# Attention's state as one plane of 64x64 tiles, the gates' chain split between VectorE and GpSimd, and another fixed order

## The chip, the cores and the metric

The kernel runs on one core of a Trainium2 chip. The metric is device time in microseconds (us) of one launch, as the median of several runs. A core has TensorE (PE; PEld is its weight load), VectorE (DVE), ScalarE (ACT), GpSimd (POOL) and SyncE (SP), which only issues DMA transfers here.

## The reference, cut to what matters

Three layers follow one another: a gated linear attention (mLSTM) over 2 batches of 8 heads with 768 steps and head size 40, then two feed-forward layers over all 1536 tokens (320 wide, 2048 and 1536 hidden).

```python
for t in range(S):                       # attention, per batch and head
    m_new = np.maximum(f_gate[:, :, t] + m, i_gate[:, :, t])
    f_stab = np.exp(f_gate[:, :, t] + m - m_new)
    i_stab = np.exp(i_gate[:, :, t] - m_new)
    m = m_new
    C = f_stab * C + i_stab * outer(vt, kt)      # state, 40 x 40
    n = f_stab * n + i_stab * kt                 # its 41st column
    h_tilde = C @ qt;  nq = n . qt
    y[t] = sigmoid(o_gate[t]) * h_tilde / max(|nq|, 1)
...
h = x @ w_in                             # layer 1
g = (a0 + a1 h + a2 h^2 + a3 h^3) / (1 + |b0| |h| + |b1| h^2 + 1e-6)
x = g @ w_out
...
xn = x / rms(x) * rms_g                  # layer 2
out = (silu(xn @ w_gate) * (xn @ w_val)) @ w_out
```

## The kernel before, in words

**Order.** The program first makes a list of small pieces by calls of `task(key, fn, deps, take, give)`; a piece has a key such as `("yi", 3)` and its instructions. Nothing is issued then. `run` (L184) walks through the hand-fixed table `ORDER`, a list of the pieces' numbers, and issues each piece's instructions. Each engine executes its own instructions in that order, so `ORDER` fixes every engine's queue and SP's queue of transfers. A piece may take a buffer from a ring and give it back; the eight PSUM banks are one ring, `"b"`, and a piece gets the bank that was given back longest ago.

**Gates.** Rows 0 to 15 and 32 to 47 of small tiles hold one row for each batch and head. The 768 steps are cut in two parts, a=0 (256 steps) and a=256 (512 steps). `gm` scans m (DVE, L423); `ga` makes two sums for the forget gate (DVE, L430 and L431); `gi` makes one for the input gate (POOL, L434); `gb` takes exponentials (ACT, L437, L438); `gc` splits the forget factor in two f16 words (DVE, L441); `gd` runs one cumulative product for each chunk of 128 steps (DVE, L449, whose second input `zc` is a zero in SBUF); `ge` transposes the result to `idt` (PE, then a copy on DVE).

**Attention** goes in 12 chunks j of 128 steps (6 for each batch). In a chunk: `s` products of k and q (PE, L504), `f` spreads the gates (PE, L484), `scan` makes the decay matrix (DVE, L487), `a` weighs the products by it (DVE, L509), `vp` and `v2` weigh v (POOL, L494, L515), `y` is the part inside the chunk (PE, L537), `yi` the part of the earlier state (PE, L527), `ys` scales that (DVE, L531), `yd` adds the two (DVE, L541), `u` is the state's growth (PE, L549), `cd` decays the state (POOL, L555), `ca` adds (DVE, L563, L565). `den0`, `den1`, `den` (ACT, POOL, DVE) make the denominators from the 41st column, `rs` and `xm` multiply (POOL), `xt`, `xh`, `xl` transpose into `xall` for layer 1. In the first chunk of a batch there is no `yi`, `ys` or `cd`, in the last one no `u`, `cd` or `ca`.

The state `cst` is a tile of 128 partitions x 4 pairs of heads x 2 planes x 41. A pair's first head has partitions 0 to 39 of plane 0, its second one partitions 64 to 103 of plane 1; all else is zero. `yi` contracts all 128 partitions, 8 products in all, with 64 columns of q as weights and both planes (82 columns) as the moving side:

```python
PE.matmul(out=t[c, 2 * p:2 * p + 2], lhsT=T("lqk", j)[:, 0, p, c], rhs=cst[:, p])
```

So the rows of the q tile between the heads have to be zero, for which `setup` clears them on POOL (L409), and the state too (L410).

**Layer 1** has 48 pairs i of (256 tokens, 256 hidden columns): `in0`, `in1` (PE, L676), a chain of elementwise pieces on ACT, DVE and POOL (`hu`, `z`, `p1`, `h2`, `zu`, `p2`, `p3`, `ars`, `sq`, `w`, `y2`, `g`, and for pairs from 16 on `gh`, `gl`), and `out0`, `out1` (PE, L681, L695, L697). Weights arrive as 64-bit words and are taken apart by `c0`, `c1`, `c2` (DVE, L331, L337, L343; `cr` on ACT and an addition on POOL for some), `hi` (ACT) and a subtraction on POOL. **Layer 2** runs in blocks of 512 or 256 tokens: `g0`, `g1` (PE, L865), `silu`, `mul`, `sh`, `sl`, and `out2` (PE, L873 to L875), then the rows go out.

## Time and profile before

| what | value |
|---|---|
| time, median of 3 runs | 481.06 us (480.97 to 481.06) |
| the profiled execution: its time, its span | 481.12 us, 479.3 us |
| PE busy | 456.4 us, 95% of the span |
| DVE, ACT, POOL busy | 331.1, 304.8, 317.5 us |
| chain of waits that ended last | PE 65%, ACT 14%, POOL 9%, DVE 8% |

The span is the time from the first to the last instruction of the program that the profile shows; the execution's own time holds 1.8 us more. Busy PE is not PE at its peak, as the ends of matmuls are modelled. An fp32 product leaves two MATMUL records, an fp32r or f16 one leaves one.

### The profile page before, as it was taken

Reading aid. Unit: us, or ns where it says so; the run is one execution under the profiler, and the core shown is the slowest. Engines: PE = TensorE matmul, PEld = TensorE weight load, DVE = VectorE, ACT = ScalarE, POOL = GpSimd, SP = SyncE. Lnnn points to the kernel's source line nnn. Section 1 sums busy time; section 2 is a strip of 40 time slices with the busy share of each in tenths; the row PEclk is TensorE's granted clock in tenths of the full one; section 3 lists DMA queues with packets and bytes.
Section 4 is the critical chain, followed back from the end, with each engine's and each line's share of the span. In section 5 each row is a group of like instructions: output and inputs, shape, how many; then the busy total and the mean of one; then the engine's idle time right before and its main releaser. Section 6 shows DMA issues by size and latency. Waiting matters only on the chain.

```text
span 479.3 us, 9356 instructions
## 1 busy us (share of the span) xinstructions
PE 456.4 (95%) x3552; PEld 414.5 (86%) x3552; DVE 331.1 (69%) x609; ACT 304.8 (64%) x576; POOL 317.5 (66%) x337
## 2 busy tenths in 40 slices
PE   3699899989999999999999999999999999999996
PEld 2588778778789999999999988888898889999996
DVE  7999999999999989899999999875210210201211
ACT  3245999999998899799999988552422212212311
POOL 5689999999998898886977778990831303213320
PEclk9998999999999999999999999999999999999999
DMA  8869371325032060010322144571100000000001
GB/s 239 273 204 255 101 196 31 114 61 143 1 102 63 1 203 3 1 42 2 115 90 83 38 160 166 180 233 59 34 15 27 1 0 2 1 27 29 1 14 57
DMA packets 18366, 40.41 MB, mean 84 GB/s; under 512 B 3952, under 2 KB 11904, under 8 KB 18320
## 3 DMA queue, kind: packets, MB, share of 16 engines
q1 hardware_dynamic: 18320, 39.80, 27.4%
q8 instruction: 28, 0.46, 0.4%
q14 instruction: 18, 0.15, 0.1%
HBM read 35.86 MB, written 3.93 MB: 83 GB/s over the span
## 4 chain that ended last, share of the span: by engine, by line
PE 65%; ACT 14%; POOL 9%; DVE 8%; issue 3%; DMA 1%; POOLq 0%; DVEq 0%; ACTq 0%
PE bank L865 26%; PE bank L676 10%; PE bank L695 5%; PE bank L875 4%; PE bank L873 4%; PE bank L874 4%; PE bank L681 4%; POOL z L720 2%; PE bank L697 2%; ACT z L710 2%; ACT u L709 2%; ACT bank L732 2%; ACT vv L718 1%; DVE w_buf L487 1%; POOL cv L356 1%
## 5 line engine op out<-in xcount | busy, mean ns | idle before, releaser
L676 PE MATMUL bank<-xall,win 128*128 128x256 f32 x768 | 104.0, 289 | 3.5 <-ACT yb L543 1.6
L676 PEld LDWEIGHTS bank<-xall,win 128*128 128x128 f32 x768 | 96.5, 193 | 7.1 <-ACT yb L543 1.8
L941 DVE TENSOR_TENSOR vv<-bank,vv 128x512 f32<-128x512 f32 x35 | 23.6, 688 | 98.0 <-PE bank L865 97.8
L720 POOL TENSOR_TENSOR z<-z,u 128x512 f32<-128x512 f32 x48 | 62.0, 1292 | 14.1 <-ACT z L710 13.1
L947 POOL TENSOR_TENSOR wou<-vv,wou 128x512 fp32r<-128x512 f32 x16 | 20.7, 1295 | 53.7 <-ACT wou L944 49.4
L938 ACT ACTIVATE vv<-bank 128x512 f32<-128x512 f32 x35 | 20.7, 595 | 50.6 <-PE bank L865 46.2
L865 PE MATMUL bank<-xall,w2gv 128*128 128x512 f32 (+1 forms) x256 | 46.4, 337 | 0.0
L749 POOL TENSOR_TENSOR gl<-vv,gh 128x512 fp32r<-128x512 f32 x32 | 41.3, 1296 | 5.6 <-ACT gh L748 3.8
L865 PEld LDWEIGHTS bank<-xall,w2gv 128*128 128x128 f32 x256 | 39.2, 190 | 4.7 <-DVE vv L739 0.2
L710 ACT ACTIVATE z<-u,few 128x512 f32<-128x512 f32 x48 | 39.2, 816 | 1.0
L695 PE MATMUL bank<-wou,gh 128*128 128x320 f32 x128 | 38.9, 316 | 0.0
L697 PE MATMUL bank<-wou,gh 128*128 128x320 f32 x128 | 38.0, 309 | 0.0
L681 PE MATMUL bank<-scr,vv 128*128 128x320 f32 x128 | 37.1, 435 | 0.0
L737 DVE SCALAR_TENSOR_TENSOR bank<-vv,few,bank 128x512 f32<-128x512 f32 x48 | 35.8, 749 | 0.0
L735 DVE SCALAR_TENSOR_TENSOR z<-z,bank 128x512 f32<-128x512 f32 x48 | 32.6, 682 | 4.4 <-ACT bank L734 3.6
L732 ACT ACTIVATE bank<-z,few 128x512 f32<-128x512 f32 x48 | 32.9, 686 | 2.5 <-DVE vv L729 2.5
L739 DVE SCALAR_TENSOR_TENSOR vv<-z,bank 128x512 f32<-128x512 f32 x48 | 32.6, 683 | 0.6
L331 DVE TENSOR_SCALAR bank<-raw 128x320 int32<-128x320 int32 x68 | 32.6, 486 | 0.3
L709 ACT ACTIVATE u<-bank 128x512 f32<-128x512 f32 x48 | 28.7, 598 | 4.0 <-POOL z L720 1.8
L865 PE MATMUL bank<-win,w2gv 128*128 128x512 f32 x128 | 31.1, 391 | 0.0
L681 PEld LDWEIGHTS bank<-scr,vv 128*128 128x128 f32 x128 | 23.2, 190 | 8.2 <-DVE vv L739 0.2
L364 POOL TENSOR_TENSOR win<-cv,win 64x128 fp32r<-64x128 f32 (+2 forms) x37 | 28.0, 757 | 2.4 <-ACT win L360 0.5
(169 smaller groups left out, 1180.3 us busy)
## 6 DMA issues: line engine op xcount, KB each, us to landing
raw<-in_w_out_dram SPq DMA_DIRECT2D x14, 640.0 KB, 4.1
raw<-in_w_gv_dram SPq DMA_DIRECT2D x12, 640.0 KB, 4.3
raw<-in_w_in_dram SPq DMA_DIRECT2D x8, 640.0 KB, 5.8
lqk<-in_qk_tr_dram SPq DMA_DIRECT2D x24, 192.0 KB, 4.7
los<-in_o_gate_dram SPq DMA_DIRECT2D x12, 160.0 KB, 3.6
lv<-in_v_dram SPq DMA_DIRECT2D x12, 160.0 KB, 4.3
lk<-in_k_dram SPq DMA_DIRECT2D x12, 160.0 KB, 3.8
z_dram<-rnd SPq DMA_DIRECT2D x6, 320.0 KB, 4.8
```

Source lines behind the costliest of these rows:

```text
L331: DVE.tensor_scalar(out=mid(x), in0=word(x, 1), scalar1=3, scalar2=0x3FFFFFFF, op0=ALU.logical_shift_left, op1=ALU.bitwise_and,)
L676: PE.matmul(out=hb()[:, e], lhsT=l, rhs=r, start=(x == 0), stop=(x == len(mm) - 1))
L681: PE.matmul(out=T("acc", n, t)[:, 0:DM], lhsT=T("vv", i)[:, e, t * 128:(t + 1) * 128], rhs=w[:, e], start=p + e == 0, stop=p == NPAIR - 1 ...
L695: PE.matmul(out=o, lhsT=l, rhs=woh[:, e], start=first, stop=last)
L697: PE.matmul(out=o, lhsT=l, rhs=wol[:, e], start=False, stop=False)
L709: go("hu", lambda: ACT.activation(out=u(), in_=hb(), func=ACTF.Abs), [("in1", i)], ["u"])
L710: go("z", lambda: ACT.activation(out=z(), in_=u(), func=ACTF.Identity, scale=babs[:, 1:2], bias=babs[:, 0:1]), [("hu", i)], ["z"])
L720: go("zu", lambda: POOL.tensor_tensor(out=z(), in0=z(), in1=u(), op=ALU.mult), [("z", i)], [], ["u"])
L732: go("ars", lambda: ACT.activation(out=hb(), in_=z(), func=ACTF.Abs_reciprocal_sqrt, bias=cq), [("zu", i), ("p3", i)])
L737: go("y2", lambda: DVE.scalar_tensor_tensor(out=hb(), in0=vv(), scalar=nacoef[:, 0:1], in1=hb(), op0=ALU.add, op1=ALU.mult), [("w", i)])
L749: go("gl", lambda: POOL.tensor_tensor(out=gl(), in0=vv(), in1=r32(gh()), op=ALU.subtract), [("gh", i)], ["gl"], ["vv"])
L865: PE.matmul(out=bank(i, e), lhsT=l, rhs=r, start=y == 0, stop=y == len(mm) - 1)
```

## The change

- **State.** `cst` becomes one plane, 128 x 4 x 41: the pair's first head on partitions 0 to 39, its second on 64 to 103. `yi` makes 16 products instead of 8, each contracting 40 partitions for one head with 64 columns of q as weights and 41 moving columns, in the four 64x64 tiles of the array; the two heads of a pair go to two PSUM banks, so `yi` takes two banks instead of one. `ys` reads them with two instructions instead of one. `u` writes 64 rows instead of 40 for each head: its weights are 64 columns of k, of which the last 24 belong to the next head (or, behind the last head, to 24 cleared columns). `cd` and `ca` become one instruction over 128 partitions instead of two over 40.
- **Cleared tiles.** The clearing of q's rows, of `cst` and of `zc` on POOL goes; two 24-column strips behind k are cleared instead.
- **Gates.** `gi` is joined to `ga`. For part a=0 all three sums run on DVE, for a=256 all three on POOL. The zero that `gd` reads moves from SBUF to a word of the PSUM bank into which `ge` of the same part transposes; DVE clears it, and `gd` takes the bank instead of `ge`.
- **Order.** `ORDER` is another list of all 1946 pieces (two `gi` fewer than before). `LAG` is 0, so `PAIRS` is the same list as before.

Read with the pieces' names, the two orders compare so (pieces that issue instructions, counted from the table; the joined `ga` counts once):

| ahead of `in0` of pair | DVE | ACT | POOL | PE | DVE's `c0`, `c1`, `scan`, `yd` |
|---|---|---|---|---|---|
| 0, before | 65 | 26 | 30 | 29 | 13, 12, 9, 2 |
| 0, after | 59 | 23 | 28 | 26 | 11, 9, 8, 3 |
| 8, before | 127 | 81 | 60 | 65 | 21, 21, 12, 4 |
| 8, after | 128 | 76 | 56 | 65 | 22, 22, 12, 4 |
| 24, before | 247 | 196 | 120 | 150 | 32, 32, 19, 7 |
| 24, after | 251 | 200 | 119 | 150 | 32, 32, 19, 7 |

Ahead of pair 8, and ahead of pair 24, PE has the same pieces in both orders, in another sequence. ACT's functions change in the order's sequence so that its table has to change 10 times before and 12 times after. The transfer of q and k for chunk 0 moves from the fourth place of SP's queue to the second, ahead of the first weights.

```diff
--- before.py
+++ after.py
@@ -20,101 +20,102 @@
 OB = [["ob"] * 4, ["raw", "raw", "raw", "ob"], ["ob", "raw"], ["ob", "cv"]]
 F_CV = [1] * 16 + [0] * 18
 NATIVE = [0, 1, 2, 3, 4, 5, 6, 7, 8, 9, 10, 11, 12, 13, 14, 15]
+LAG = 0
 BY_SQUARE = [0, 2, 4, 6, 8, 10, 12, 14, 16, 18, 20, 22, 24, 26, 28]
 ORDER = [
...
 ]
 
 
@@ -162,7 +163,8 @@
 
     BLOCKS = [(0, 2 * BLK), (2 * BLK, 2 * BLK), (4 * BLK, BLK), (5 * BLK, BLK)]
 
-    PAIRS = [(n, p) for p in range(NPAIR) for n in range(2)] + [(n, p) for n in range(2, NB) for p in range(NPAIR)]
+    PAIRS = [(n, x - n * LAG) for x in range(NPAIR + LAG) for n in range(2) if 0 <= x - n * LAG < NPAIR]
+    PAIRS += [(n, p) for n in range(2, NB) for p in range(NPAIR)]
     FINAL = [max(i for i, x in enumerate(PAIRS) if x[0] == n) for n in range(NB)]
 
     PE, ACT, DVE, POOL = nc.tensor, nc.scalar, nc.vector, nc.gpsimd
@@ -265,13 +267,12 @@
     dexp = at.tile([48, NCH, BH // 2], FP32, name="dexp")
     idt = at.tile([128, NCH, 48], FP32, name="idt")
     dl = at.tile([128, NCH, BH // 2], FP32, name="dl")
-    cst = at.tile([128, HP, 2, D1], FP32, name="cst")
-    zc = at.tile([48, 1], FP32, name="zc")
+    cst = at.tile([128, HP, D1], FP32, name="cst")
     den = at.tile([128, H, 1], FP32, name="den")
-    for nm, n in (("k", 2), ("v", 2)):
-        ring("l" + nm, tiles(at, n, [128, H, D], FP32, "l" + nm))
-    qk_bufs = tiles(at, 2, [128, 2, HP, L], FP32, "lqk")
-    ring("lqk", qk_bufs)
+    ring("lv", tiles(at, 2, [128, H, D], FP32, "lv"))
+    lk_bufs = tiles(at, 2, [128, H * D + 64 - D], FP32, "lk")
+    ring("lk", lk_bufs)
+    ring("lqk", tiles(at, 2, [128, 2, HP, L], FP32, "lqk"))
     ring("yb", tiles(at, 2, [128, H, D1], FP32, "yb"))
 
 
@@ -282,7 +283,10 @@
     def load(i, nm):
         if nm != "qk":
             src = {"k": k, "v": v, "o": o_gate}[nm][i * L:(i + 1) * L].rearrange("p (h d) -> p h d", h=H)
-            nc.sync.dma_start(out=lo_of(i) if nm == "o" else T("l" + nm, i), in_=src)
+            dst = lo_of(i) if nm == "o" else T("l" + nm, i)
+            if nm == "k":
+                dst = dst[:, 0:H * D].rearrange("p (h d) -> p h d", h=H)
+            nc.sync.dma_start(out=dst, in_=src)
             return
         for e in range(2):
             nc.sync.dma_start(
@@ -403,11 +407,8 @@
         DVE.memset(g48, 0.0)
         DVE.memset(cq, 1.0 + 1e-6)
         DVE.memset(eps6, 1e-6)
-        POOL.memset(zc, 0.0)
-        for t in qk_bufs:
-            for r0 in (32, 96):
-                POOL.memset(t[r0:r0 + 32, 0], 0.0)
-        POOL.memset(cst, 0.0)
+        for t in lk_bufs:
+            POOL.memset(t[:, H * D:], 0.0)
         for nm, dst, src in (
             ("eye", ident, eye4[:, 0:128]), ("eye4", id4, eye4), ("sel", sel, pick), ("hv", hv[FR], halves),
             ("pb", bcoef, pb[None, :].to_broadcast([128, 2])), ("pa", acoef, pa[None, :].to_broadcast([128, 4])),
@@ -426,12 +427,11 @@
         )
 
     def gate_a(a, b):
-        gf = gate_in[:, 0, a:b]
-        DVE.tensor_tensor(out=gf, in0=gf, in1=m_t[:, a:b], op=ALU.add)
-        DVE.tensor_tensor(out=g48[FR, a:b], in0=gf, in1=m_t[:, a + 1:b + 1], op=ALU.subtract)
-
-    def gate_i(a, b):
-        POOL.tensor_tensor(out=g48[0:BH, a:b], in0=gate_in[:, 1, a:b], in1=m_t[:, a + 1:b + 1], op=ALU.subtract)
+        e = POOL if a else DVE
+        gf, m1 = gate_in[:, 0, a:b], m_t[:, a + 1:b + 1]
+        e.tensor_tensor(out=gf, in0=gf, in1=m_t[:, a:b], op=ALU.add)
+        e.tensor_tensor(out=g48[FR, a:b], in0=gf, in1=m1, op=ALU.subtract)
+        e.tensor_tensor(out=g48[0:BH, a:b], in0=gate_in[:, 1, a:b], in1=m1, op=ALU.subtract)
 
     def gate_b(a, b):
         ACT.activation(out=g48[:, a:b], in_=g48[:, a:b], func=ACTF.Exp)
@@ -444,9 +444,11 @@
         DVE.memset(f16[:, a:b].rearrange("p (c l) -> p c l", l=L)[:, :, 0:1], 0.0)
 
     def gate_d(a, b):
+        zc = T("gt", a)[FR, 511:512]
+        DVE.memset(zc, 0.0)
         for c in range(a // L, b // L):
             sl = g48[FR, c * L:(c + 1) * L]
-            DVE.tensor_tensor_scan(out=sl, data0=sl, data1=zc[FR].to_broadcast([BH, L]), initial=1.0, op0=ALU.mult, op1=ALU.add)
+            DVE.tensor_tensor_scan(out=sl, data0=sl, data1=zc.to_broadcast([BH, L]), initial=1.0, op0=ALU.mult, op1=ALU.add)
 
     def gate_e(a, b):
         c0, c1 = a // L, b // L
@@ -521,14 +523,22 @@
             return T(name, j)[:, 0:H * D1].rearrange("p (h d) -> p h d", h=H)
 
         def yi():
-            t = heads("pi")
             for p in range(HP):
                 for c in (slice(0, 64), slice(64, 128)):
-                    PE.matmul(out=t[c, 2 * p:2 * p + 2], lhsT=T("lqk", j)[:, 0, p, c], rhs=cst[:, p])
+                    for e in range(2):
+                        r = slice(64 * e, 64 * e + D)
+                        PE.matmul(out=odd(e)[c, p], lhsT=T("lqk", j)[r, 0, p, c], rhs=cst[r, p])
+
+        def odd(e):
+            return T("pi", j, e)[:, 0:HP * D1].rearrange("p (a b) -> p a b", a=HP)
 
         def ys():
-            dd = idt[:, ch, 32 + b * H:32 + (b + 1) * H][:, :, None].to_broadcast([128, H, D1])
-            DVE.tensor_tensor(out=T("yb", j), in0=heads("pi"), in1=dd, op=ALU.mult)
+            dd = idt[:, ch, 32 + b * H:32 + (b + 1) * H].rearrange("p (a e) -> p a e", e=2)
+            for e in range(2):
+                DVE.tensor_tensor(
+                    out=T("yb", j).rearrange("p (a e) d -> p a e d", e=2)[:, :, e], in0=odd(e),
+                    in1=dd[:, :, e:e + 1].to_broadcast([128, HP, D1]), op=ALU.mult,
+                )
 
         def y():
             t = heads("py")
@@ -546,23 +556,18 @@
             t = T("pu", j)[:, 0:HP * D1].rearrange("p (a b) -> p a b", a=HP)
             for h in range(H):
                 r0 = 64 * (h % 2)
-                PE.matmul(out=t[r0:r0 + D, h // 2], lhsT=T("lk", j)[:, h], rhs=v2_buf[:, h])
+                PE.matmul(out=t[r0:r0 + 64, h // 2], lhsT=T("lk", j)[:, h * D:h * D + 64], rhs=v2_buf[:, h])
 
         def cd():
-            for e in range(2):
-                r = slice(64 * e, 64 * e + D)
-                dd = dl[r, ch, b * HP:(b + 1) * HP][:, :, None].to_broadcast([D, HP, D1])
-                POOL.tensor_tensor(out=cst[r, :, e, 0:D1], in0=cst[r, :, e, 0:D1], in1=dd, op=ALU.mult)
+            dd = dl[:, ch, b * HP:(b + 1) * HP][:, :, None].to_broadcast([128, HP, D1])
+            POOL.tensor_tensor(out=cst, in0=cst, in1=dd, op=ALU.mult)
 
         def ca():
             t = T("pu", j)[:, 0:HP * D1].rearrange("p (a b) -> p a b", a=HP)
-            for e in range(2):
-                r = slice(64 * e, 64 * e + D)
-                cc = cst[r, :, e, 0:D1]
-                if ch:
-                    DVE.tensor_tensor(out=cc, in0=t[r], in1=cc, op=ALU.add)
-                else:
-                    DVE.tensor_copy(out=cc, in_=t[r])
+            if ch:
+                DVE.tensor_tensor(out=cst, in0=t, in1=cst, op=ALU.add)
+            else:
+                DVE.tensor_copy(out=cst, in_=t)
 
         def den_(x):
             if x == 0:
@@ -612,8 +617,10 @@
             ("v2", j), None if last else v2, [("scan", j, 0), ("scan", j, 1), ("vp", j)] + prev("u")
         )
         if ch:
-            task(("yi", j), yi, [("s", j), ("ca", j - 1)], take=[key_(("pi", j))], give=[("lqk", j)])
-            task(("ys", j), ys, [("yi", j), ("gates", ch)], take=[("yb", ("yb", j))], give=[("pi", j)])
+            task(("yi", j), yi, [("s", j), ("ca", j - 1)], take=[key_(("pi", j, e)) for e in range(2)],
+                 give=[("lqk", j)])
+            task(("ys", j), ys, [("yi", j), ("gates", ch)], take=[("yb", ("yb", j))],
+                 give=[("pi", j, e) for e in range(2)])
         task(("y", j), y, [("a", j, 0), ("a", j, 1), ("vp", j)], take=[key_(("py", j))])
         task(
             ("yd", j), yd, [("y", j)] + ([("ys", j)] if ch else []),
@@ -984,13 +991,11 @@
 
             go("gm", lambda a=a, b=b: gate_m(a, b),
                [("ld", "gates")] + ([("gm", parts[x - 1][0])] if x else []))
-            go("gi", lambda a=a, b=b: gate_i(a, b), [("gm", a)])
             go("ga", lambda a=a, b=b: gate_a(a, b), [("gm", a)])
-            go("gb", lambda a=a, b=b: gate_b(a, b), [("ga", a), ("gi", a)])
+            go("gb", lambda a=a, b=b: gate_b(a, b), [("ga", a)])
             go("gc", lambda a=a, b=b: gate_c(a, b), [("gb", a)])
-            go("gd", lambda a=a, b=b: gate_d(a, b), [("gc", a)])
-            go("ge", lambda a=a, b=b: gate_e(a, b), [("gd", a), ("ld", "eye")], take=[("b", ("gt", a))],
-               give=[("gt", a)])
+            go("gd", lambda a=a, b=b: gate_d(a, b), [("gc", a)], take=[("b", ("gt", a))])
+            go("ge", lambda a=a, b=b: gate_e(a, b), [("gd", a), ("ld", "eye")], give=[("gt", a)])
             for c in range(a // L, b // L):
                 task(("fgates", c), None, [("gc", a), ("ld", "sel"), ("ld", "eye4")])
                 task(("gates", c), None, [("ge", a)])
```

## Rows read from the trace of the kernel before

**Rows 1.** Windows: length, busy us of PE, PEld, DVE, ACT, POOL.
```profile
0.00:15.40 15.40, 4.92 (x29) 3.88 (x29) 12.38 (x25) 5.04 (x9) 7.75 (x14) 1.00 0.89 246
15.40:44.90 29.50, 26.45 (x331) 22.95 (x330) 28.54 (x59) 13.63 (x30) 25.15 (x39) 0.98 0.78 240
44.90:60.00 15.10, 13.65 (x149) 12.49 (x148) 14.25 (x26) 12.65 (x24) 14.04 (x22) 0.93 0.47 133
60.00:120.00 60.00, 56.20 (x432) 46.44 (x429) 57.19 (x101) 57.78 (x102) 58.39 (x58) 1.00 0.37 109
120.00:300.00 180.00, 179.54 (x1519) 165.51 (x1518) 170.27 (x308) 165.93 (x321) 151.29 (x155) 1.00 0.23 71
300.00:475.64 175.64, 175.60 (x1106) 163.19 (x1104) 48.50 (x95) 49.33 (x95) 60.88 (x53) 1.00 0.14 45
```

**Rows 2.** Timeline of PE (start us, us, what): layer 1's first pair.
```profile
44.90 3.16 PE L676 MATMUL bank<-xall,win 128*128 128x256 f32 x16
```

**Rows 3.** Timeline of DVE, 3 to 16.5 us: the gates' chain.
```profile
5.24 0.78 DVE L430 TENSOR_TENSOR scr<-scr 16x256 f32<-16x256 f32 x1
6.05 1.20 DVE L431 TENSOR_TENSOR scr<-scr 16x256 f32<-16x256 f32 x1
7.28 0.68 DVE L430 TENSOR_TENSOR scr<-scr 16x512 f32<-16x512 f32 x1
7.99 0.68 DVE L431 TENSOR_TENSOR scr<-scr 16x512 f32<-16x512 f32 x1
...
10.04 0.41 DVE L441 SCALAR_TENSOR_TENSOR f<-scr,f 16x256 f16<-16x256 f32 x1
...
10.61 0.73 DVE L449 TENSOR_TENSOR_SCAN scr<-scr,zc 16x128 f32<-16x128 f32 x2
...
12.72 2.65 DVE L449 TENSOR_TENSOR_SCAN scr<-scr,zc 16x128 f32<-16x128 f32 x4
```

**Rows 4.** Timeline of POOL, 3 to 20 us: what ran beside rows 3.
```profile
4.25 2.71 POOL L434 TENSOR_TENSOR scr<-scr 16x256 f32<-16x256 f32 x2
12.83 1.63 POOL L356 TENSOR_TENSOR cv<-cv,rnd 128x640 int32<-128x640 int32 x1 [5.86 <-DVE cv L337]
```

**Rows 5.** Groups by shape: count, busy us, mean ns, idle before.
```profile
L331 DVE TENSOR_SCALAR bank<-raw 128x320 int32<-128x320 int32 x68 | 32.6, 486 | 0.3
...
L563 DVE TENSOR_TENSOR cst<-bank,cst 40x164 f32<-40x164 f32 x16 | 5.2, 322 | 0.8 <-PE bank L549 0.6
L531 DVE TENSOR_TENSOR yb<-bank,idt 128x328 f32<-128x328 f32 x10 | 4.9, 491 | 0.7 <-PE bank L527 0.6
...
L487 DVE TENSOR_TENSOR_SCAN w_buf<-bank,id 128x512 f32<-128x512 f32 x24 | 29.1, 1215 | 0.8 <-PE bank L484 0.5
...
L555 POOL TENSOR_TENSOR cst<-cst,dl 40x164 f32<-40x164 f32 x16 | 7.4, 460 | 0.6
```

**Rows 6.** Groups of PE between 120 and 300 us, which hold five chunks.
```profile
L681 PE MATMUL bank<-scr,vv 128*128 128x320 f32 x36 | 10.3, 435 | 0.0
L504 PE MATMUL bank<-lqk 40*128 40x128 f32 x80 | 5.8, 285 | 0.0
L537 PE MATMUL bank<-vp_buf,scr 128*64 128x41 f32 x160 | 5.7, 231 | 0.0
L527 PE MATMUL bank<-cst,lqk 128*64 128x82 f32 x80 | 4.0, 240 | 0.0
...
L549 PE MATMUL bank<-v_buf,lk 128*40 128x41 f32 x80 | 2.5, 206 | 0.0
```

**Rows 7.** Timeline of PE's weight loads in an early chunk.
```profile
27.82 0.62 PEld L549 LDWEIGHTS bank<-v_buf,lk 128*40 128x40 f32 x16 [0.20 <-issue]
...
28.32 1.83 PEld L537 LDWEIGHTS bank<-vp_buf,scr 128*64 128x64 f32 x32
...
30.79 1.11 PEld L527 LDWEIGHTS bank<-cst,lqk 128*64 128x64 f32 x16 [0.64 <-DVE cst L563]
```

**Rows 8.** Timeline of ACT, 0 to 280 us: a change of its table.
```profile
99.70 1.28 ACT L732 ACT_TABLE_LOAD   x1
```

186 rows, old and new, of the table ORDER are left out of this document.

## The prediction

> **What bounds the kernel now.** The profile was read from the coarse to the fine: the page, windows over the whole span, the chain of waits, and then the early timeline. The windows carry the argument [rows 1]. From 300 us to the last product at 475.64 us TensorE is busy for 175.60 of 175.64 us and the others for about a third of it: layer 2 is a string of products, and nothing in this change touches it. Between 120 and 300 us PE is again busy for 179.54 of 180 us, with VectorE at 170.27 and ScalarE at 165.93: PE sets the pace, the others follow closely. Ahead of 120 us it is another matter. PE has few products in the first 15.4 us (4.92 us busy), and what it then does between 15.4 and 44.9 us is chunks of attention at about half its later pace: a weight load of `y` takes 1.83 us for 32 [rows 7], 57 ns each, while five chunks' 160 records of `y` take 5.7 us after 120 us [rows 6], 36 ns each. VectorE is what is full there: 28.54 of 29.5 us, then 14.25 of 15.1 and 57.19 of 60 [rows 1]; GpSimd is as full between 60 and 120 us (58.39 of 60). The first pair's product starts at 44.90 us [rows 2]. So the end is the length of PE's products plus the time that PE loses early, and the early loss is VectorE's: a microsecond of VectorE's work that goes from ahead of the first pairs lets the products start earlier by about as much, while after 120 us only PE's own work counts.
>
> The profiled execution took 481.12 us; its span is 479.3 us, and the last product is followed by 3.7 us of copying and storing that the change keeps. The median of the runs is 481.06 us, so sums on this execution hold for the median.
>
> **The gates.** `ga` and `gi` of part 0 now run on VectorE with nothing on GpSimd beside them. Before, the two sums of part 0 took 0.78 and 1.20 us and those of the longer part 0.68 each, 3.34 us in all [rows 3]; a two-input instruction over the same 16x256 that ran alone took 0.41 [rows 3]. Three of these are 1.24 us: 2.1 us saved, since the longer part leaves VectorE. The slow ones ran beside GpSimd's two subtractions [rows 4]. The six cumulative products took 0.73 us for two and 2.65 for four [rows 3]; the four ran beside an addition of 1.63 us on GpSimd [rows 4]. At the price of the first two, 0.37 each, six are 2.2 us, 1.2 less than now; as they now read their zero from PSUM I expect no such wait. Two clearings of a word are added; one of `f16` now fits into the 0.16 us between the end of the row at 10.04 and the row at 10.61 [rows 3], so I take +0.1 for both. Against this: GpSimd now has three sums of the longer part, 4.1 us at the mean of its two in rows 4, and `gc` of part 0 comes on VectorE in that time, with both inputs in SBUF. It costs between nothing and one such sum (1.4 us); I take 0.8, since `gc` will come somewhere in the middle of one. Behind `gc` stand `gd`, the first scans and with them the whole of chunk 0.
>
> The slow rows have one thing in common: two SBUF inputs on VectorE while GpSimd reads SBUF. The Trainium skill, page SBUF — State Buffer, section Who interferes with whom, says that such instructions exclude each other for a whole instruction. This trace agrees with 1.20 us for a sum whose like takes 0.41; by the page's rule the wait of `gc` would be up to the rest of the GpSimd instruction under way, so the rule speaks against putting part 256 on GpSimd, but only once.
>
> **The state.** `ca` becomes one instruction: 0.322 us less in a chunk [rows 5], as 40 and 128 partitions are one row of lanes. `ys` becomes two over 164 elements each, at 0.322 instead of one at 0.491 [rows 5]: +0.15. Up to pair 8 five chunks have both: -1.6 and +0.8. `cd` saves 0.46 us of GpSimd in a chunk [rows 5]; GpSimd is full from 60 us on, but VectorE is as full beside it, so I count it at nothing of its own; without it, GpSimd could take back 1.8 us, its four `cd` ahead of pair 8. The clearings of q and of `cst` went on while GpSimd was still waiting for its first input (it idled for 5.86 us ahead of the addition in rows 4), so nothing.
>
> **The order.** PE has the same 65 pieces ahead of pair 8 in both orders. VectorE has one `c0` and one `c1` more there, 0.49 us each [rows 5]: +1.0. The lead at pair 8 is then 2.1 + 1.2 - 0.1 - 0.8 + 1.6 - 0.8 - 1.0 = 2.2 us. Ahead of pair 0 it is larger: two `c0`, three `c1` and a scan (1.215 us [rows 5]) fewer, one `yd` more (priced as `ys`): 3.2 us, plus the edits' 2.1 + 1.2 - 0.1 - 0.8 + three times 0.17 = 2.9, so 6.1 us. The six microseconds are partly borrowed, for the deferred pieces come back ahead of pair 8. Ahead of pair 24 PE's list is equal again, and VectorE has four pieces more, but there PE is the one that decides. I take the lead at pair 8.
>
> **PE's own work.** `yi` goes from 16 records to 32, with 41 instead of 82 columns. Now a chunk's `yi` is 0.80 us and its `y`, with as many records, as many columns and 64 weight columns too, 1.14 us [rows 6]. If the four tiles work two at a time, as in `y`, the new one costs 1.14; if four at a time, half of that, 0.57. Two at a time is what rows show for both directions: per column a record of `s` (two row tiles) takes 72/128 = 0.57 ns and one of `yi` (two column tiles) 50/82 = 0.61, where the whole array takes 286/320 = 0.89 [rows 6]. Since both directions overlap by themselves I take 0.70 us, nearer to four: -0.1 in a chunk. `u` loads 64 instead of 40 columns: 57 instead of 39 ns for each of 16 early loads [rows 7], +0.29 us early and about half of it later; by rows 6 (36 instead of 31 ns) +0.08. I take +0.1. The two cancel; the bounds are -0.2 and +0.5 us in a chunk, so -1.1 and +2.5 us for the five chunks behind 120 us.
>
> The Trainium skill, TensorEngine Tiling (Array Packing), section Tiling Modes, counts four independent tiles of 64x64 that load and multiply in parallel. By it `yi` would be at the 0.57 us end. No run shown so far has such tiles.
>
> **The sum.** 481.1 - 2.2 + 0 = 478.9; I say **479.0 us**. After 120 us I add nothing: PE now loses 0.46 us of 180 there.
>
> **Rivals.** (A) The whole 6.1 us of pair 0 survives, because the deferred splitting of weights fits into gaps: 481.1 - 6.1 = 475.0. For it speaks that ScalarE is only half busy until 44.9 us (13.63 of 29.5); against it, that all of VectorE, ScalarE and GpSimd are over 95% busy from 60 to 120 us [rows 1]. (B) The other side: the tiles of `yi` go two at a time. Then each late chunk costs 0.5 us more (2.5), and early ones, where 32 loads of 57 ns replace 1.11 us and `u` adds 0.29 [rows 7], up to 1.0 us each for the three ahead of pair 0, of which I let half count: 481.1 - 2.2 + 2.5 + 1.5 = 482.9, slower. It decides once a late `yi` takes over 1.0 us. For it: no row shows four at once. (C) `gc` waits for two of GpSimd's sums and not for part of one: 2.7 instead of 0.8 us, lead gone, 480.8, no change. Against it: a single sum lost 0.8 us in rows 3. (D) ScalarE or an in-order queue takes the lead back. Two more table changes are 2.6 us [rows 8] on an engine that is busy for 57.78 of 60 us: 478.9 + 2.6 = 481.5, no change; with PE's queue behind a late product some more, up to 483. `yi` takes two banks, and by counting through the table 58 takes, not 48, get the last free bank. Against it: the extra loads fall behind pair 16, where ScalarE has 14 us of slack in 180.
>
> **Chances.** Forecast, 477.5 to 480.1: 0.42. A, below that: 0.15. B: 0.18. C: 0.10. D: 0.15, two thirds of it within 0.2%, the rest slower. A difference of 0.2%, 1 us, is about what a measurement of this kernel can tell from none. So faster 0.57, same 0.20, slower 0.23. The range takes in A's full lead and B, 475.0 to 483.2.
>
> **What would show it.** Right: the first `scan` ahead of 13 us instead of behind the last row of rows 3, at 15.4, cumulative products of 0.4 us each, the first product of pair 0 near 39 to 42 us, VectorE still over 95% busy until 120 us, PE without gaps behind it, a late `yi` of 0.6 to 0.8 us. Wrong: `yi` at 1.1 us (B), a `gc` of over 1.5 us (C), or PE idle for over 3 us between 120 and 300 us (D). The prediction fails most easily in the order, of which I have priced only what stands ahead of pairs 0 and 8.

## The result, and the profile after

The changed kernel takes 476.04 us (median of 4 runs, 475.63 to 476.68) against 481.02 (4 runs) for the kernel before: a ratio of 0.9897, 95% interval 0.9885 to 0.9909, so 5.0 us less. Forecast were 2.1 less. The direction and the start of pair 0 came as forecast; the sum was too small by 2.9 us. The profiled execution of the changed kernel took 475.63 us, with a span of 473.9. From its page, the busy time of each engine:

```profile
PE 457.1 (96%) x3712; PEld 417.0 (88%) x3712; DVE 324.5 (68%) x610; ACT 307.2 (65%) x578; POOL 312.2 (66%) x326
```

The windows of the changed kernel (columns as in [rows 1]; the cuts are its own first and last products):

```profile
0.00:15.40 15.40, 7.79 (x54) 6.48 (x54) 12.03 (x29) 4.16 (x6) 7.53 (x14) 1.00 0.91 250
15.40:38.87 23.47, 22.56 (x331) 20.31 (x330) 22.12 (x49) 11.07 (x25) 18.72 (x31) 1.00 0.81 258
38.87:60.00 21.13, 18.66 (x212) 16.59 (x211) 20.19 (x40) 18.90 (x35) 20.27 (x24) 1.00 0.62 183
60.00:120.00 60.00, 58.66 (x445) 48.02 (x445) 56.89 (x100) 56.20 (x97) 57.91 (x59) 1.00 0.30 91
120.00:300.00 180.00, 178.96 (x1593) 166.16 (x1592) 170.27 (x313) 172.10 (x332) 150.52 (x154) 1.00 0.26 80
300.00:470.46 170.46, 170.46 (x1088) 159.40 (x1086) 42.98 (x84) 44.38 (x85) 57.29 (x49) 1.00 0.12 39
```

Against [rows 1]: nothing is won behind 120 us, where PE idles for 1.04 us in 180 instead of 0.46. Between 60 and 120 us it loses 1.34 us instead of 3.80, so 2.5 us come from there, a stretch that the forecast had left to "VectorE is as full". The rest is what remains of the earlier start, in the timeline of PE:

```profile
38.87 1.44 PE L683 MATMUL bank<-xall,win 128*128 128x256 f32 x5
```

Pair 0 starts 6.0 us ahead of [rows 2]. How the lead then goes, from the first products of the pairs in the traces (us):

| kernel | pair 0 | pair 8 | pair 24 | last product ends |
|---|---|---|---|---|
| before | 44.9 | 81.2 | 163.0 | 475.6 |
| changed | 38.9 | 78.2 | 158.3 | 470.5 |
| lead | 6.0 | 3.0 | 4.7 | 5.1 |
| before's instructions, new order | 44.0 | 85.4 | 165.4 | 477.9 |

Half of the six microseconds is handed back by pair 8 (forecast were 3.9 of 6.1); then the lead grows again, which was not forecast. The timeline of VectorE shows the gates' chain of the changed kernel, which answers [rows 3]:

```profile
4.25 0.41 DVE L432 TENSOR_TENSOR scr<-scr 16x256 f32<-16x256 f32 x1
4.70 0.42 DVE L433 TENSOR_TENSOR scr<-scr 16x256 f32<-16x256 f32 x1
5.14 0.41 DVE L434 TENSOR_TENSOR scr<-scr 16x256 f32<-16x256 f32 x1
...
6.79 0.41 DVE L441 SCALAR_TENSOR_TENSOR f<-scr,f 16x256 f16<-16x256 f32 x1
...
7.48 0.73 DVE L451 TENSOR_TENSOR_SCAN scr<-scr,bank 16x128 f32<-16x128 f32 x2
...
9.57 2.33 DVE L489 TENSOR_TENSOR_SCAN w_buf<-bank,id 128x512 f32<-128x512 f32 x2
...
13.55 1.36 DVE L451 TENSOR_TENSOR_SCAN scr<-scr,bank 16x128 f32<-16x128 f32 x4
```

and the timelines of GpSimd and ScalarE what ran beside it ([rows 4]):

```profile
6.84 1.48 POOL L432 TENSOR_TENSOR scr<-scr 16x512 f32<-16x512 f32 x1 [5.29 <-DVE scr L424]
8.40 1.08 POOL L433 TENSOR_TENSOR scr<-scr 16x512 f32<-16x512 f32 x1
9.56 1.08 POOL L434 TENSOR_TENSOR scr<-scr 16x512 f32<-16x512 f32 x1
```

```profile
0.71 1.28 ACT L437 ACT_TABLE_LOAD   x1 [0.71 <-PEq L1094]
```

The three sums take 0.41 us each and the cumulative products 0.37 and 0.34, as forecast. `gc` (L441) took 0.41: it started 0.05 us ahead of GpSimd's first sum and did not wait, so that the 0.8 us that the forecast had charged for it came to nothing. The first scan starts at 9.57 us instead of 15.40. One thing was not foreseen: ScalarE's table for the exponential, loaded at 7.33 us before, behind the wait for the sums, now is loaded at 0.71, so that 1.28 us are out of ScalarE's part of the chain.

The groups by shape, late on PE ([rows 6]) and on VectorE over the whole span ([rows 5]):

```profile
L547 PE MATMUL bank<-vp_buf,scr 128*64 128x41 f32 x160 | 5.7, 231 | 0.0
L530 PE MATMUL bank<-cst,lqk 40*64 40x41 f32 x160 | 3.4, 230 | 0.0
L559 PE MATMUL bank<-v_buf,lk 128*64 128x41 f32 x80 | 3.3, 233 | 0.0
```

```profile
L538 DVE TENSOR_TENSOR yb<-bank,idt 128x164 f32<-128x164 f32 x20 | 5.5, 318 | 0.3 <-PE bank L530 0.2
L568 DVE TENSOR_TENSOR cst<-bank,cst 128x164 f32<-128x164 f32 x8 | 2.6, 321 | 0.0
```

`yi` is 3.4 us for five chunks, 0.68 each (0.80 before, 0.70 forecast), `u` 0.66 (0.50 before): together +0.04 us in a chunk. `ca` and `ys` cost what rows 5 said of their shapes.

### The profile page after: what moved, and what is told of

The parts are those of the page before. It is cut to its first block, busy times and chain, and to the rows that moved or that the text cites. A ratio compares the mean times of both kernels' runs of the same rounds, so it can differ in the third digit from the quotient of the medians.

```text
span 473.9 us, 9691 instructions
## 1 busy us (share of the span) xinstructions
PE 457.1 (96%) x3712; PEld 417.0 (88%) x3712; DVE 324.5 (68%) x610; ACT 307.2 (65%) x578; POOL 312.2 (66%) x326
## 4 chain that ended last, share of the span: by engine, by line
PE 67%; POOL 11%; DVE 9%; ACT 8%; issue 3%; DMA 1%; DVEq 0%; POOLq 0%; ACTq 0%
PE bank L872 28%; PE bank L683 10%; PE bank L702 7%; PE bank L882 4%; PE bank L881 4%; PE bank L880 4%; PE bank L704 3%; POOL z L727 2%; DVE w_buf L489 2%; POOL win L368 2%; POOL vv L729 1%; POOL cv L360 1%; POOL wou L368 1%; ACT bank L739 1%; PE bank L547 1%
## 5 line engine op out<-in xcount | busy, mean ns | idle before, releaser
L954 POOL TENSOR_TENSOR wou<-vv,wou 128x512 fp32r<-128x512 f32 x18 | 23.2, 1295 | 55.2 <-ACT wou L951 49.5
```

## The experiments

All were timed in five rounds against the kernel before. The first columns are the median and the ratio with its interval; the last one is the difference of the medians from the kernel that the experiment starts from. The changed kernel and its variants were timed at different times, each beside the kernel before; by the two ratios the seven rows that start from it would read +4.4, +3.9, +3.5, +2.3, +2.5, +4.3 and, for `less_pool`, +0.9. Each ratio's interval reaches 0.4 to 1.0 us to either side, so differences of less than 1 us between two such rows are not clear of noise.

| kernel | us | ratio to before | 95% interval | starts from | difference, us |
|---|---|---|---|---|---|
| new_order | 483.32 | 1.0041 | 1.0029 to 1.0053 | before | +2.2 |
| new_instr | 481.75 | 1.0011 | 0.9996 to 1.0026 | before | +0.7 |
| gates_old_order | 479.73 | 0.9969 | 0.9957 to 0.9981 | before | -1.4 |
| state_old_order | 483.23 | 1.0040 | 1.0025 to 1.0054 | before | +2.1 |
| old_gates | 480.86 | 0.9988 | 0.9976 to 1.0000 | changed | +4.8 |
| old_gates_early | 479.90 | 0.9979 | 0.9971 to 0.9988 | changed | +3.9 |
| zero_in_sbuf | 479.85 | 0.9970 | 0.9958 to 0.9982 | changed | +3.8 |
| old_state | 478.69 | 0.9944 | 0.9922 to 0.9965 | changed | +2.7 |
| decay_halves | 478.57 | 0.9949 | 0.9936 to 0.9962 | changed | +2.5 |
| exp_early | 481.00 | 1.0004 | 0.9996 to 1.0013 | before | 0.0 |
| more_pool | 485.43 | 1.0089 | 1.0068 to 1.0109 | before | +4.4 |
| more_dve | 483.39 | 1.0043 | 1.0029 to 1.0057 | before | +2.4 |
| more_act | 483.50 | 1.0046 | 1.0031 to 1.0062 | before | +2.5 |
| more_pe | 483.44 | 1.0044 | 1.0030 to 1.0058 | before | +2.4 |
| pool_in_after | 480.43 | 0.9986 | 0.9978 to 0.9995 | changed | +4.4 |
| less_pool | 477.36 | 0.9916 | 0.9903 to 0.9929 | changed | +1.3 |
| less_pool_filled | 477.41 | 0.9914 | 0.9895 to 0.9933 | less_pool | +0.1 |
| decay_halves_filled | 478.51 | 0.9940 | 0.9924 to 0.9956 | decay_halves | -0.1 |

**Order or instructions.** Two kernels hold one half of the change each. `new_order` has the instructions of before in the sequence of the new table, with `gi` right behind `ga`; `new_instr` has the new instructions in the old sequence, where only ten pieces around chunk 4's `yi` stand as `xh` 3, `xl` 3, `yi` 4, `hu` 0, `z` 0, `p3` 0, `zu` 0, first `scan` 5, `in0` 1, `in1` 1, so that two banks are free for `yi`. The tables' first numbers in the former and, below, in the latter:

```diff
 ORDER = [
-    0, 8, 19, 9, 374, 10, 21, 375, 376, 377, 3, 20, 36, 11, 2, 12, 13, 22, 23, 39, 26, 378, 15, 24, 41, 42, 45, 46, 1,
+    0, 8, 10, 9, 11, 19, 36, 374, 12, 13, 375, 376, 377, 3, 2, 15, 41, 42, 43, 4, 17, 45, 46, 1, 14, 16, 62, 67,
...
-    0, 8, 9, 10, 18, 34, 372, 11, 12, 373, 374, 375, 3, 2, 14, 39, 40, 41, 4, 16, 43, 44, 1, 13, 15, 60, 65, 66, 410,
+    0, 8, 18, 372, 9, 19, 373, 374, 375, 3, 34, 10, 2, 11, 12, 20, 21, 37, 24, 376, 14, 22, 39, 40, 43, 44, 1, 13,
```

> The instructions of the kernel before in the new order, with the gates' third sum on GpSimd right behind the other two. First theory, the order carries the gain, since it puts fewer of GpSimd's and VectorE's pieces ahead of the first pairs: 477 to 478.5 us. Second theory, the edits carry it, since they shorten the gates' chain and the state's work, and the order is only another one of equal worth: 480 to 482 us.

> The new instructions in the old order of each engine (only PSUM banks are handed out in a slightly different sequence around chunk 4). First theory, order: 479.5 to 481 us. Second theory, edits: 476.5 to 478 us. If both parts count and add up, the two gains sum to 5 us.

The order alone is 2.2 us slower, the instructions alone 0.7 (an interval that holds no change): neither half brings anything, and together they bring 5.0. Both medians lie outside all that I had expected. So I took the changed kernel and put the old gates' chain (`old_gates`) or the old state in two planes (`old_state`) back into it, in the new order (the diff shows the gates; the state's is the change's own, reversed):

```diff
-        e = POOL if a else DVE
-        e.tensor_tensor(out=gf, in0=gf, in1=m_t[:, a:b], op=ALU.add)
-        e.tensor_tensor(out=g48[FR, a:b], in0=gf, in1=m1, op=ALU.subtract)
-        e.tensor_tensor(out=g48[0:BH, a:b], in0=gate_in[:, 1, a:b], in1=m1, op=ALU.subtract)
+        DVE.tensor_tensor(out=gf, in0=gf, in1=m_t[:, a:b], op=ALU.add)
+        DVE.tensor_tensor(out=g48[FR, a:b], in0=gf, in1=m1, op=ALU.subtract)
+        POOL.tensor_tensor(out=g48[0:BH, a:b], in0=gate_in[:, 1, a:b], in1=m1, op=ALU.subtract)
...
-            DVE.tensor_tensor_scan(out=sl, data0=sl, data1=zc.to_broadcast([BH, L]), initial=1.0, op0=ALU.mult, op1=ALU.add)
+            DVE.tensor_tensor_scan(out=sl, data0=sl, data1=zc[FR].to_broadcast([BH, L]), initial=1.0, op0=ALU.mult, op1=ALU.add)
```

> The kernel after with the gates' chain as before (two sums on VectorE and one on GpSimd for both parts, the zero in SBUF). If the chain's 2 to 3 us at the start last to the end: 478 to 479 us. If they are covered by what follows: 476 to 477 us.

> The kernel after with the state as before (two planes, eight products over 128 rows, two instructions for the decay and for the addition, q's rows cleared), gates and order new. If GpSimd's shorter decay and VectorE's shorter addition are worth their time: 477.5 to 479 us. If TensorE's changed products and the two-bank yi cost as much as these save: 475.5 to 476.5 us.

In the new order the gates are worth 4.8 us and the state 2.7; their sum, 7.5, is about what lies between `new_order` and the changed kernel (483.32 - 476.04 = 7.28). The gates had been expected to be worth 3 us at most. Nearly half of what they bring to the start of pair 0 is a wait that goes, and not work. Of VectorE's waits up to 38 us in `old_gates` (us in total, times, longest):

```profile
DVE f L442 <- ACT f L439: 2.5, 2, 1.4
```

There `gc` of both parts stands until ScalarE has made the exponentials, for 1.03 and 1.42 us; in the changed kernel, and in the kernel before with its other order, VectorE does not wait for them.

**The same two in the old order.** `gates_old_order` is before with the new gates alone, `state_old_order` before with the new state alone (and the ten pieces as above).

> New gates, old state, old order. Theory 1 (the edits' lead of 2.6 us at pair 0 was spent in the old order by the new state, whose `yi` takes two banks of the ring): 478.5 to 479.2 us, a lead of some 2.5 us that is still there at pair 8. Theory 2 (the old order itself gives an early gates' chain nothing, since other engines' pieces are due at places that suit a late start): within 0.5 us of the kernel before, the lead of pair 0 gone by pair 8.

> Old gates, new state, old order (the ten pieces around chunk 4's `yi` in the sequence that leaves two banks free). Theory 1 (the two-bank `yi` costs what the gates had gained): 1.5 to 3 us above the kernel before, most of it between pairs 0 and 8. Theory 2 (the old order gives neither edit anything): 481 to 482 us.

Theory 1 holds in kind: -1.4 and +2.1 add up to the +0.7 of `new_instr`. In size it misses for the gates: 479.73 us lies between the two theories, and pair 0 starts 1.2 us earlier, not 2.6. The timelines of VectorE and GpSimd in `gates_old_order` show why:

```profile
5.10 0.39 DVE L406 TENSOR_TENSOR scr<-scr 16x256 f32<-16x256 f32 x1
5.52 1.37 DVE L407 TENSOR_TENSOR scr<-scr 16x256 f32<-16x256 f32 x1
6.90 1.22 DVE L408 TENSOR_TENSOR scr<-scr 16x256 f32<-16x256 f32 x1
```

```profile
5.25 1.35 POOL L406 TENSOR_TENSOR scr<-scr 16x512 f32<-16x512 f32 x1 [1.08 <-DVE scr L398]
6.68 1.16 POOL L407 TENSOR_TENSOR scr<-scr 16x512 f32<-16x512 f32 x1
```

The old order has `gm` of both parts first, so the three sums of part 0 run beside GpSimd's sums of part 256 and take 2.98 us instead of the 1.24 of the changed kernel, where they are over before GpSimd starts.

Where the state loses is in the timeline of PE in `state_old_order`, at chunk 4's `yi` (L508) and pair 1 (L661), and in what its engines waited for between 45 and 60 us (us in total, times, longest):

```profile
51.24 0.31 PE L508 MATMUL bank<-cst,lqk 40*64 40x41 f32 x2
52.10 0.67 PE L508 MATMUL bank<-cst,lqk 40*64 40x41 f32 x30 [0.55 <-DVE xall L638]
53.98 4.39 PE L661 MATMUL bank<-xall,win 128*128 128x256 f32 x19 [1.21 <-DVE w_buf L467]
```

```profile
POOL z L705 <- ACT z L695: 4.1, 2, 3.4
DVE vv L712 <- ACT vv L703: 2.8, 1, 2.8
ACT u L694 <- PE bank L661: 2.4, 1, 2.4
```

The first two products of `yi` write its first bank; the rest waits until `xl` has read out another one, and pair 1 then waits for the bank that a scan still reads. In `gates_old_order`, with `yi` in one bank, `yi` and pair 1 follow each other there without a gap. In these two waits TensorE loses 1.8 us here, and the others wait 2.4 to 4.1. The granted clock is 0.50 for 6.8 us from 52.7 us on, where the second of these waits begins, and this execution is the slowest of its kernel (484.38 us, the others 481.71 to 483.31). So that the bank alone makes the 2.1 us is read from the waits and not shown; no run has the new state in the old order with a bank to spare.

**Which term.** Three kernels undo one detail each in the changed kernel: `zero_in_sbuf` reads the zero of the cumulative products from SBUF as before; `old_gates_early` is `old_gates` with part 256's `ga` right behind its `gm`; `decay_halves` makes `cd` in two instructions. `exp_early` gives the kernel before a small exponential at the start, which brings its table load to 0.72 us. The edits in turn (`old_gates_early` only moves one number in the table):

```diff
-        zc = T("gt", a)[FR, 511:512]
-        DVE.memset(zc, 0.0)
...
-            dd = dl[:, ch, b * HP:(b + 1) * HP][:, :, None].to_broadcast([128, HP, D1])
-            POOL.tensor_tensor(out=cst, in0=cst, in1=dd, op=ALU.mult)
+            for r in (slice(0, 64), slice(64, 128)):
+                dd = dl[r, ch, b * HP:(b + 1) * HP][:, :, None].to_broadcast([64, HP, D1])
+                POOL.tensor_tensor(out=cst[r], in0=cst[r], in1=dd, op=ALU.mult)
...
+        ACT.activation(out=few[:, 14:15], in_=eps6, func=ACTF.Exp)
```

> The kernel after, with the zero of the cumulative products back in SBUF and all else new. Theory, the early chain lasts to the end: one product waits for a GpSimd instruction, 1.3 us, and the time is 477 to 477.5 us. Rival, the wait is covered: 475.8 to 476.4 us.

> The kernel after with the old gates' chain as in the first such run, but with the sums of the long part right behind its scan, as the order before had them, and not 25 places later. If the 4.8 us of that run came from the edit of the gates itself: 480 to 481 us again. If they came from an order that fits only the new chain, most comes back: 477 to 479 us.

> The kernel after with the state's decay in two instructions over 64 partitions each, 0.46 us more of GpSimd in each of eight chunks, 3.7 us in all, 1.8 of it ahead of pair 8. The prediction's step (GpSimd's time counts nothing of its own): 475.8 to 476.5 us. Rival, GpSimd sets the pace until about 105 us: 477.3 to 478 us.

> The kernel before plus one exponential of a single constant at the very start on ScalarE, so that its table is loaded while the gates are still on their way. If the 1.3 us that this takes out of the gates' chain last to the end: 479.5 to 480 us. If the old order doesn't use them: 480.8 to 481.3 us.

The zero alone is 3.8 of the gates' 4.8 us. The timeline of VectorE in `zero_in_sbuf`:

```profile
7.36 2.41 DVE L451 TENSOR_TENSOR_SCAN scr<-scr,zc 16x128 f32<-16x128 f32 x2
...
14.99 3.15 DVE L451 TENSOR_TENSOR_SCAN scr<-scr,zc 16x128 f32<-16x128 f32 x4
```

Beside the first of them GpSimd makes the same three sums of part 256 as in the changed kernel (6.84 to 10.66 us). The same six products take 5.56 us instead of 2.09, and pair 0 starts at 42.9 us instead of 38.9. These 4.0 us are still 4.1 at pair 8, 4.2 at pair 24 and 4.3 at the end: an early delay here goes through to the end. I had expected one product to wait, 1.3 us. `old_gates_early`, between its two branches, is the same within 0.05 us: with the zero in SBUF and the sums at an early place, which engine makes them, with a table load at 5.48 us instead of 0.71, is worth nothing that shows. The other microsecond of `old_gates` would be the late place of part 256's sums; the intervals of these two kernels overlap, so it is not clear of noise.

`decay_halves` costs 2.5 us, above its rival's range and as much as the whole old state. So of the state's edits, GpSimd's one instruction less in a chunk is what counts (16 of 456 ns in place of 8 of 465, 3.6 us in all); `ca`, `ys`, `yi` and `u` together are worth nothing that shows. `exp_early` brings nothing, as its second branch had it: the exponentials of part 0 end at 8.08 us instead of 9.48, but `gc` starts at 9.91 instead of 10.04, since in VectorE's queue part 256's sums and three instructions of weight splitting stand ahead of it; the first scan still starts at 15.3 us.

**The price of a microsecond.** Four kernels add some 3 us of work between pairs 0 and 8 of the kernel before (GpSimd's second addition is just behind pair 8), by doing an instruction twice that writes the same values again: `more_pool` the low halves of `w_out` 0 and 1, `more_dve` chunk 5's scans and one `a`, `more_act` `hu` of pairs 1 to 5, `more_pe` `in1` of pairs 1 to 3. `pool_in_after` does to the changed kernel what `more_pool` does to before, and `less_pool` has VectorE make those two subtractions there:

```diff
+            for _ in range(2 if key in (("o", 0), ("o", 1)) else 1):
...
+          for _ in range(2 if j == 5 else 1):
...
+        go("hu", lambda: [ACT.activation(out=u(), in_=hb(), func=ACTF.Abs) for _ in range(2 if 1 <= i <= 5 else 1)],
...
+        go("in1", lambda: [inp(1) for _ in range(2 if 1 <= i <= 3 else 1)], [("in0", i)])
...
-            for v, hi, lo in dst(r32(cv())):
-                POOL.tensor_tensor(out=lo, in0=v, in1=r32(hi), op=ALU.subtract)
+            eng = DVE if key in (("o", 0), ("o", 1)) else POOL
+            for v, hi, lo in dst(r32(cv())):
+                eng.tensor_tensor(out=lo, in0=v, in1=r32(hi), op=ALU.subtract)
```

> The kernel before with two of GpSimd's subtractions (low words of w_out 0 and 1) made twice, 3.1 us more on GpSimd between about 70 and 90 us. The prediction's step, that GpSimd's time counts nothing of its own while VectorE is as full: 481 to 481.8 us. Rival, that GpSimd sets the pace between pairs 2 and 12: 483 to 484.2 us.

> The kernel before with both scans and one weighing of chunk 5 made twice, 3.1 us more on VectorE between about 54 and 70 us. The prediction's step, that a microsecond of VectorE ahead of the first pairs is a microsecond of the end: 483.5 to 484.2 us. Rival, that GpSimd or ScalarE sets the pace there: 481 to 482.3 us.

> The kernel before with the absolute value of pairs 1 to 5 made twice, 3.0 us more on ScalarE between about 56 and 75 us. If VectorE or GpSimd alone sets the pace: 481 to 482 us. If all three engines are links of one chain there: 482.5 to 484 us.

> The kernel before with the second half of the products of pairs 1 to 3 made twice, 2.9 us more on TensorE between about 53 and 62 us. The prediction's step, that TensorE has room there: 481 to 482 us. If TensorE's sequence sets the end from the first pairs on: 483.5 to 484 us.

> The changed kernel with the low halves of `w_out` 0 and 1 subtracted twice (3.1 us more of GpSimd between pairs 2 and 8; the second pass writes the same values). If GpSimd's work sets the early pace in the new order too, as it did before (1.4 us for each): 3.1 to 4.4 us more, 479.1 to 480.4 us, the whole of it there at pair 8. If the new order has given GpSimd slack: under 1 us more, 476 to 477 us.

> The changed kernel with the same two subtractions on VectorE in GpSimd's place: 3.1 us off GpSimd, at about 0.7 us each 1.4 us on VectorE. If GpSimd is the dearest engine early (1.4 us for 1 against VectorE's 0.76): -4.4 + 1.1 = some 3 us less, of which waits for GpSimd's instruction under way (up to 1.6 us for each of the two, as both operands lie in SBUF) may take back 1 to 2: 473 to 475 us. If VectorE is the limit: 1 us or more above the changed kernel, 477 us.

For 1 us more the time grows by 4.4/3.1 = 1.4 us on GpSimd (more than either branch of `more_pool`), 2.4/3.1 = 0.8 on VectorE, 2.5/3.0 = 0.8 on ScalarE and 2.4/2.9 = 0.8 on TensorE. No engine has slack there, and in the changed kernel GpSimd's price is the same 1.4. That it is higher than the others' is not GpSimd's time alone. The profiled `pool_in_after`, 4.65 us behind the changed kernel in the end, is 0.8 us behind at pair 8 (I had expected the whole there) and 4.9 at pair 12. Between them VectorE waits once 2.57 us for GpSimd, and then TensorE, in its timeline here, with the same eight records in the changed kernel last:

```profile
90.71 0.48 PE L507 MATMUL bank<-lqk 40*128 40x128 f32 x2 [1.95 <-DVE scr L341]
91.90 1.16 PE L507 MATMUL bank<-lqk 40*128 40x128 f32 x14 [0.71 <-DVE vv L747]
...
93.60 4.11 PE L689 MATMUL bank<-scr,vv 128*128 128x320 f32 x8
```

```profile
89.94 2.42 PE L688 MATMUL bank<-scr,vv 128*128 128x320 f32 x8
```

Behind its waits TensorE ran at a granted clock of 0.50, its lower level of 1.2 GHz, for 3.4 us from 93.9 us on, and these eight records took 1.7 us more. `more_pool` has the same 3.4 us at 0.50 from 95.7 us on. Without these 1.7 us GpSimd's price in `pool_in_after` would be near 1; this is an estimate from the trace, and no run here keeps the clock up at that place.

The price holds in one direction only: `less_pool` takes 3.1 us off GpSimd, VectorE makes the two subtractions in 0.82 and 1.03 us,

```profile
69.46 0.82 DVE L369 TENSOR_TENSOR wou<-scr,wou 128x640 fp32r<-128x640 f32 x1
```

and the kernel is 1.3 us slower (0.9 by the two ratios), 0.7 for each of VectorE's 1.85 us, as if GpSimd's relief were worth nothing. My reckoning of 3 us less failed; 477 us was the other branch, VectorE as the limit.

**The clock.** In `less_pool` and `decay_halves` TensorE idles for 1.6 us near 53 us, and then the granted clock falls to 0.50, its lower level of 1.2 GHz, for some us. Two kernels put products into that idle time: chunk 5's four products of `f` for the first gates are made four times.

```diff
-            for e in range(4):
+            for e in 4 * [0, 1, 2, 3] if (j, g) == (5, 0) else range(4):
```

> The two subtractions on VectorE as in less_pool, and the four products that spread chunk 5's first gates (0.39 us) are made four times in a row, the same values into the same bank: some 1.2 us of products in the 1.63 us in which TensorE stood idle at 52.6 us of less_pool, just ahead of 3.4 us at a granted clock of 0.50 to 0.66. Theory (the price of an early delay holds a part of the clock: an idle stretch of TensorE is followed by some us at half the clock): the granted clock stays at 1.00 behind 54 us and 1 to 1.7 us come back, 475.7 to 476.4 us. Rival (the lower clock there costs nothing, since other engines set the pace): 477.4 us as less_pool, or a little more, whatever the clock shows.

> The state's decay in two instructions as in decay_halves, with the same four products made four times, in the 1.65 us in which TensorE stood idle at 54.0 us of decay_halves, ahead of a granted clock of 0.50 to 0.91 in 56 to 62 us. Theory: the clock stays up there and 1 to 1.7 of the 2.5 us that the second instruction cost come back, 476.9 to 477.6 us. Rival (all 2.5 us are GpSimd's time on the chain): 478.6 us.

The windows of PE (busy us, granted clock) in `decay_halves`, and below them in `decay_halves_filled`:

```profile
54.00:56.00 2.00, 0.35 (x13) 1.00 0.82 312
56.00:58.00 2.00, 2.00 (x36) 0.74 1.06 224
58.00:60.00 2.00, 2.00 (x11) 0.50 1.05 233
```

```profile
54.00:56.00 2.00, 2.00 (x40) 1.00 0.88 310
56.00:58.00 2.00, 2.00 (x43) 1.00 1.05 218
58.00:60.00 2.00, 2.00 (x17) 1.00 0.87 186
```

The filled stretch keeps 1.00, and pair 4 starts at 61.3 us instead of 62.5. By pair 8 nothing of that is left (80.4 against 80.5), and the time is the same. The clock did fall in that execution too, but earlier, at 48 to 54 us. So the rival holds: in this stretch other engines set the pace, and the lower clock is not the price (at 94 us, above, products did take longer, and nothing was tried). Another pair of windows of the same two kernels says so more plainly, `decay_halves` first:

```profile
28.00:42.00 14.00, 13.69 (x183) 0.50 0.84 249
```

```profile
28.00:42.00 14.00, 13.76 (x182) 1.00 0.86 260
```

Fourteen microseconds of attention at half the clock, and pair 0 starts at 39.60 us instead of 39.45. The five executions of `decay_halves` say the same: the profiled one has a mean clock of 0.975, the others 0.995 or 0.996, and all take 478.5 to 478.6 us. `less_pool_filled` decides nothing: 0.97 us of idle time remained, and the clock fell again.

## Why the prediction was wrong by size

**Where the missing 2.9 us are.** The forecast closed its sum at pair 8, with a lead of 2.2 us. In the traces the lead is 3.0 us there and 5.1 at the last product. So 2.2 of the 2.9 us come behind pair 8, for which the sum has nothing: its step "there PE is the one that decides. I take the lead at pair 8" failed. That it was only 0.8 off at pair 8 is luck: the edits are worth 7.1 us there in the new order where the sum has 3.2, and the order alone costs 4.2 where it has 1.0 (`new_order` against the changed kernel and the kernel before).

**Its working on the start was right.** Pair 0 was to start 6.1 us earlier and starts 6.0 earlier. Ahead of it VectorE is busy for 34.15 us instead of 40.92 and idle for 4.7 instead of 4.0, so its work did set the start, as the prediction has it. The sums, the products, `yi`, `ca` and `ys` have the durations forecast, and `u` 0.16 us more where 0.1 was forecast. But the two halves do not add up: in `new_order` VectorE is busy for 36.90 us up to pair 0 and yet the pair starts only 0.9 us earlier, as VectorE is idle for 7.0 us, 2.5 of them for the exponentials.

Rival B falls with a late `yi` of 0.68 us, where two tiles at a time would be 1.14. The Trainium skill, TensorEngine Tiling (Array Packing), section Tiling Modes, counts four independent tiles of 64x64, by which it would be 0.57, an estimate with half of the 1.14; the trace comes within 0.11 us of that. Rival C falls with `gc` at 0.41 us. Of D, ScalarE's two more table changes came (12 against 10), but PE idles only 0.6 us more behind 120 us. A named nearly the right time, 475.0, for another reason: half of pair 0's lead was handed back, not kept.

**Step "there PE is the one that decides. I take the lead at pair 8".** From pair 8 to pair 24 the new order gains: 1.8 us in the changed kernel (2.98 to 4.74), 1.8 in `new_order` (4.15 behind to 2.33). Before, TensorE waits in that stretch, at 102 us, for an in-order copy on ScalarE (waits of PE in the kernel before, 99 to 106 us):

```profile
PE bank L676 <- ACT yb L543: 1.6, 1, 1.6
```

Ahead of that copy stands the table load of [rows 8], 1.28 us; the changed kernel has no table load between 48.3 and 140.7 us, and no such wait. `gates_old_order`, with the old order, has the load at 98.2 us, the same wait of 1.6 us and, like the kernel before, 81.8 us from pair 8 to pair 24, where `new_order` and the changed kernel take 80.0 and 80.1. So the wait goes with the order; that the load is what made PE wait is read from the chain of waits, not tried. The remaining 0.4 us, behind pair 24, was not taken apart.

**Step "`cd` saves 0.46 us of GpSimd in a chunk [...] I count it at nothing of its own".** It is worth 2.5 us in the changed order (`decay_halves`), 2.3 of them at pair 8. Behind it stood "VectorE is what is full there": the four price runs refute that this is all, as a microsecond on any engine costs 0.8 us or more. That GpSimd was busy for 58.39 of 60 us stood in [rows 1] and in the prediction itself.

**Step "VectorE has one `c0` and one `c1` more there [...] +1.0".** This term for the order is too small, which hid at pair 8 how much the edits brought: with the instructions of before the new order is 4.2 us behind at pair 8 and 2.2 at the end. Its chunk 1 scans at 20.8 us, where the changed kernel does at 16.4: the sequence is laid out for gates that are ready earlier.

**Step "six are 2.2 us, 1.2 less than now".** This term came as forecast against the kernel before (2.09 us, 1.3 less), but not for its reason alone. I took the saving from rows where two of the products ran undisturbed and four beside one addition. The change itself puts three sums on GpSimd beside the first two; beside them and with the zero in SBUF the six take 5.56 us, and the end is 3.8 us later (`zero_in_sbuf`). Without the PSUM zero, moving part 256 to GpSimd would have gained nothing (`old_gates_early` takes the same time). The Trainium skill, SBUF — State Buffer, section Who interferes with whom, says that a VectorE instruction with two SBUF inputs contends with a GpSimd instruction that reads SBUF. The trace agrees for the cumulative products: 2.41 us against 0.73 for the same two.

Each taken from the kernel that undoes it in the new order, the terms come near the whole: zero 3.8, late place of the sums 1.0, `cd` 2.5, the rest of the state 0.1, the order -2.2: 5.2 us, against 5.0 measured. The forecast had 3.2 for the edits and -1.0 for the order.

What stays open: why nothing comes back when 1 us of GpSimd is taken away, how much of the 1.4 us for an added one is the clock, and whether `yi`'s second bank alone makes the +2.1 of the state in the old order. That the gates are worth 4.8 us in one order and 1.4 in the other is in the traces: with the new order the old gates add 2.5 us of waits for the exponentials, and in the old order the new ones lose 1.7 us in sums beside GpSimd's.

## What to carry to other kernels

Where the order of all engines is fixed by hand, an edit has no price of its own: the same new state cost 2.1 us in the old order, where its `yi` had to wait for a second PSUM bank, and saved 2.7 in an order that had a place for it. Price an edit against the neighbours that the change gives it, not those in the trace of before, and charge early work on every engine that is over 95% busy, not only on the one that looks fullest. A lead at one point says little of the end; look at the next places where PE idles, and ask whether the new order still has them.
